# Attention, gated layers and a SiLU layer on one core: sums, low halves and normalising of the opening moved to GpSimd, with a new opening order

## The chip, the cores and the metric

One core of a Trainium2 chip. The metric is the device time in microseconds (us) of one execution, from its first to its last instruction with what lies around it. The engines are TensorE (PE, with its weight loads PEld), VectorE (DVE), ScalarE (ACT), GpSimd (POOL) and SyncE (SP), which issues the loads and stores.

## The reference

Three stages in a row, all in 32-bit floats. B = 4, H = 8 heads, S = 576 positions, head size 64.

```python
# 1. attention
q_d, k_d, v_d = means over 4 neighbouring positions of q, k, v     # 144 positions
out_d     = softmax(q_d @ k_d.T / 8) @ v_d                          # coarse
scores    = where(|i - j| < 4, q @ k.T / 8, -1e9)
out_local = softmax(scores) @ v                                     # local
x = (repeat(out_d, 4) + out_local)        # reshaped to 2304 tokens x 512
# 2. gated layer: w1, w2 512 x 1024, w3 1024 x 1024, w_out 1024 x 512
x = ((x @ w1) * (x @ w2)) @ w3 @ w_out
# 3. SiLU layer: w_in 512 x 2048, w_out 2048 x 512
h = x @ w_in;  y = (h * sigmoid(h)) @ w_out
```

Softmax subtracts the row's maximum and divides by the sum plus 1e-9.

## The kernel before

**Units.** The attention is done in 16 units u, each one batch entry and a pair of heads. A unit loads its q and k (`qk`, 579 KB, L289), a version of v cut into windows (`vw`, two loads, 200 and 160 KB, L296) and v for the coarse part (`vr`, 320 KB, L302). Its steps have names in the order list, the unit's number last:
- coarse part: `pq` sums q and k over four positions (DVE, L309); `sd` scores (PE, L351); `md` negated maximum (DVE, L359, L361); `xd` three exponentials (ACT, L323) into tile Ed; `rd` the inverse of the sums (DVE, two small steps, L330 and L333); `nd` normalising of Ed (L338 on ACT or L340 on GpSimd); `td0`, `td1` transposes (PE, L401); `cd` copies of them (ACT); `pv0`, `pv1` v's pooled sums (L437, L444); `od` the product with v (PE, L453); `os` its copy out of PSUM (DVE, L461).
- local part: `s` scores of 64 queries by 38 keys, 72 small products in the records (PE, L376); `mk` adds the mask (DVE, L386) into the one tile `band`; `ml` the maximum (DVE, L390) and its scaled negative (L392); `x0` to `x2` nine exponentials (ACT, L323); `rl` inverse (DVE); `n0` to `n2` normalising of band; `tl0` to `tl2` transposes (PE, L423) and `cl` copies; `ol` the product with the windows of v (PE, L475).
- `xf` adds the two (DVE, L488), `xh` takes the high half of the sum as FP32R (ACT, L501) and `xo` subtracts it to get the low half (L505): products of the later stages are made of passes over high and low halves.

**Weights.** w3 and w_out are not applied one after the other: their product is made first, in 64 products `pGHT` of 128x128 by 128x512 (PE, L592, tiles `wp`; two records each in the trace), and cast into w_wC (L601, L606). Weights lie in memory as 64-bit floats. Each piece (`o0` to `o3` of w_out, `t00` to `t13` of w3, `w12_0` to `w12_7` of w1 and w2 side by side) is loaded in two halves of 512 KB (`Lw...`, L221) and decoded in four steps: `a` on ACT (L174, 0.67 us for half a piece), `d1` clamp (DVE, L179), `d2` shift (DVE, L185), `d3` join (DVE, L191). A w12 piece then gets a high half (`h`, ACT, L265) and a low half (`l`, DVE, L268), tiles w_wA and w_wB.

**Opening.** Units 0 to 4 and most of unit 5, the 64 products, the decoding and the first products of the gated layer (`ab`, L640) stand in one list, `OPENING`, written out by hand (L38 to L71): each engine, and SP with its loads, works off its own instructions in this order, one after the other. At most eight loads are on their way at once. While the list runs, `side()` is DVE and `norm` works slice by slice on ACT; behind it `side()` is GpSimd, and `norm` is one GpSimd instruction. So in the opening GpSimd has nothing to do after making the mask. `KEYS` is the order in which the weight pieces claim buffers, `CUTS` the pieces whose first parts are cut smaller. Idle products (L126) on a zeroed tile stand ahead of everything on PE (NWARM of them) and, as `z0` and `z1`, in the list.

**After the opening** the units 6 to 15 are interleaved with the gated layer, and then the SiLU layer runs over all tokens. The change touches there only `mk`, `ml` and the scale of `x0` to `x2`.

Of the kernel before, what the change touches and what calls it, by code (L numbers as in the profile page):

```python
# [35 lines left out]


OPENING = """  # L38
Lwt000 Lwt001 Lwt002 Lq0 Lwo00 Lwo01 Lwt010 Lwt011 at00a d2t00a Lwo10 d1t00a Lwo11 at00b d3t00a
d2t00b d1t00b d3t00b Lva0 at00c d2t00c d1t00c d3t00c Lvb0 s0 pq0 Lr0 ao0a d2o0a sd0 z0 z1 mk0  # L40
ml0 Lq1 ao0b d1o0a d3o0a x00 md0 p000 Lwo20 x10 d1o0b p001 d2o0b xd0 d3o0b Lq2 p002 d2t01 x20
p003 rd0 Lwo21 at01 rl0 p004 p005 nd0 d1t01 Lwt020 p006 d3t01 Lwt021 n00 Lwo30 td00 n10 d2o1
td10 Lwo31 p007 n20 pv00 ao1 pv10 Lwt030 pq1 s1 cd00 cd10 tl00 tl10 d1o1 Lr1 cl00 sd1 cl10 d3o1
tl20 od0 Lwt031 cl20 md1 p010 os0 xd1 pq2 p011 Lq3 ao2 p012 d2o2 Lwt100 p013 rd1 mk1 nd1 p014
d1o2 Lwt101 d3o2 sd2 at02 d2t02 s2 Lww12_00 md2 p015 d1t02 p016 Lww12_01 d3t02 ao3 p017 ml1 ol0
Lq4 d1o3 x01 Lwt110 p020 pv01 x11 pv11 p021 d2o3 Lva1 x21 d3o3 p022 at03 p023 rl1 Lr2 d2t03 p024
n01 d1t03 n11 p025 d3t03 Lvb1 n21 p026 pq3 p027 Lwt111 p030 d2t10 at10 xf00 p031 Lww12_20 xf10
xh00 td01 d1t10 xh10 td11 cd01 d3t10 Lww12_21 p032 cd11 xd2 tl01 d2w12_0 tl11 p033 xo00 cl01 rd2
cl11 tl21 xo10 aw12_0 p034 mk2 ml2 od1 cl21 wh00 d1w12_0 p035 nd2 wl00 p036 os1 wh01 d3w12_0
p037 x02 ol1 wl01 wh02 wh03 pv02 p100 x12 wl02 Lva2 Lvb2 wl03 p101 x22 xf01 p102 xf11 hw12_0 rl2  # L50
td02 pv12 td12 n02 d2t11 Lr3 p103 n12 lw12_0 p104 n22 d2w12_2 sd3 xh01 xh11 xo01 cd02 s3 xo11
cd12 md3 tl02 at11 Lq5 tl12 pq4 p105 cl02 p106 cl12 aw12_2 d1t11 tl22 d3t11 od2 cl22 xd3 p107
os2 Lwt120 d1w12_2 p110 Lwt121 d3w12_2 sd4 rd3 ol2 Lww12_30 hw12_2 mk3 Lww12_31 ml3 nd3 p111
lw12_2 Lva3 Lvb3 x03 p112 xf02 p113 x13 xf12 pv03 td03 x23 d2t12 td13 p114 pv13 at12 md4 Lr4
p115 rl3 xh02 d1t12 s4 xh12 n03 d3t12 p116 Lq6 n13 p117 xo02 Lwt130 n23 xo12 Lwt131 p120 d2w12_3
cd03 cd13 pq5 p121 xd4 tl03 tl13 pv04 aw12_3 p122 rd4 p123 cl03 d1w12_3 cl13 nd4 tl23 d3w12_3
od3 p124 cl23 os3 Lww12_10 hw12_3 mk4 p125 Lww12_11 ml4 at13 p126 lw12_3 p127 x04 d1t13 ol3 x14
d2t13 d3t13 x24 sd5 Lva4 Lvb4 pv14 s5 Lww12_50 rl4 Lr5 xf03 aw12_1 p130 Lq7 d2w12_1 Lww12_51
td04 xf13 n04 p131 d1w12_1 n14 d3w12_1 td14 n24 p132 md5 cd04 p133 Lww12_40 cd14 Lww12_41 hw12_1
tl04 tl14 p134 cl04 lw12_1 cl14 tl24 xh03 p135 wh10 xo03 cl24 od4 mk5 wh11 wl10 p136 xh13 aw12_5  # L60
wl11 p137 os4 xo13 wh12 ab000a d1w12_5 wh13 ab000b wl12 xd5 ab000c wl13 ab001a af00 d2w12_5
ab001b aw12_4 ab001c d3w12_5 ab010a ab010b cf00 Lww12_60 hw12_5 ab010c cc00 Lww12_61 d1w12_4
ab011a co00 af01 ab011b lw12_5 ab011c ab020a d2w12_4 ab020b cf01 ab020c cc01 ab021a d3w12_4 af02
co01 ab021b ab021c rd5 Lww12_70 hw12_4 d2w12_6 ab030a Lww12_71 cf02 ab030b aw12_6 cc02 ab030c
lw12_4 co02 ab031a nd5 ab031b d1w12_6 af03 ab031c d3w12_6 ab040a ab040b cf03 ab040c hw12_6 cc03
ab041a ml5 co03 ab041b af04 lw12_6 aw12_7 ab041c ab050a x05 cf04 ab050b cc04 ab050c x15 d1w12_7
co04 ab051a d2w12_7 af05 ab051b x25 d3w12_7 ab051c ab060a cf05 ab060b hw12_7 cc05 ab060c rl5
ab061a co05 af06 lw12_7 ab061b n05 ab061c n15 ol4 cf06 n25 cc06 ab070a co06 Lva5 xf04 ab070b
Lvb5 xf14 xh04 ab070c xh14 xo04 ab071a af07 xo14 ab071b ab071c ab100a cf07 ab100b cc07 ab100c
ab101a co07 af10 ab101b ab101c cf10 cc10 co10  # L70
""".split()  # L71


# [1107 lines left out]
```

## Time and profile before

| | |
|---|---|
| median of 3 runs | 843.88 us (843.46 to 847.28) |
| profiled execution, its own time | 843.95 us |
| its span in the trace | 842.1 us |
| granted TensorE clock, mean | 1.00 (2.4 GHz) |
| PE busy | 831.4 us, 99% of the span |
| DVE, ACT, GpSimd busy | 494.7, 304.0, 270.7 us |

The trace is of one execution. "Busy" counts the time in which an engine works on an instruction, waiting left out; what an engine waits for is in the views of waits, and in square brackets behind a row of the timeline. Times on the axis count from the span's start.

### The profile page before, as it was taken

The page shows a single profiled execution, that of the slowest core. Times are in us where ns is not written, and L with a number is a line of the kernel's source. Part 1 is how long each engine was busy: PE and PEld are TensorE (multiplying, and loading weights), DVE is VectorE, ACT ScalarE, POOL GpSimd, SP SyncE. Part 2 cuts the span into 40 slices and gives each one's busy share as a digit, 9 for nine tenths or more (in the row PEclk, how much of TensorE's full clock was granted, in tenths as well). Part 3 has the DMA queues.
Part 4 walks back from the last instruction along what each step waited for, and adds up shares of the span by engine and source line. Part 5 has one row for each costly group of instructions (what it writes and reads, how often), then busy time and mean ns, then how long its engine had stood idle before and what let it go on. Part 6 is the DMA issues. An engine that isn't in the chain of part 4 may idle for free.

```text
span 842.1 us, 17446 instructions
## 1 busy us (share of the span) xinstructions
PE 831.4 (99%) x7126; PEld 737.6 (88%) x7126; DVE 494.7 (59%) x833; ACT 304.0 (36%) x881; POOL 270.7 (32%) x216
## 2 busy tenths in 40 slices
PE   8999999999999999999999999999999999999997
PEld 4555798999999999999999998999999998988986
DVE  7999896666455737356952543447544537534434
ACT  6598665544444435433432111123111123211111
POOL 3000233453434534231451432435232435221220
PEclk9999999999999999999999999999999999999999
DMA  9978755446455543518951783542762432832502
GB/s 312 378 196 262 228 169 166 143 154 225 159 206 170 192 168 106 200 59 288 369 197 35 282 302 140 182 181 87 214 199 88 148 115 87 236 102 89 168 6 76
DMA packets 44032, 149.16 MB, mean 177 GB/s; under 512 B 9136, under 2 KB 15792, under 8 KB 37808
## 3 DMA queue, kind: packets, MB, share of 16 engines
q1 hardware_dynamic: 43952, 148.05, 52.0%
q8 instruction: 56, 0.92, 0.5%
q14 instruction: 24, 0.20, 0.1%
HBM read 115.52 MB, written 32.51 MB: 176 GB/s over the span
## 4 chain that ended last, share of the span: by engine, by line
PE 94%; DMA 3%; DVE 2%; issue 0%; SPq 0%; ACT 0%
PE o L986 24%; PE ab L640 23%; PE h L1075 21%; PE y L705 12%; PE wp L592 5%; PE ol L475 2%; PE sd L351 1%; PE tl L423 1%; PE s L376 1%; DMA qk<-qk 1%; PE td L401 1%; PE od L453 1%; DMA st<-w 1%; DMA lent<-wo 1%; DVE w_wA L268 0%
## 5 line engine op out<-in xcount | busy, mean ns | idle before, releaser
L986 PE MATMUL o<-wo,g 128*128 128x512 f32 x864 | 221.1, 393 | 0.0
L986 PEld LDWEIGHTS o<-wo,g 128*128 128x128 f32 x864 | 160.7, 188 | 25.4
L1039 POOL TENSOR_TENSOR g<-sg,g 128x768 fp32r<-128x768 f32 x46 | 84.9, 1846 | 228.4 <-DVE g L1037 217.3
L1075 PE MATMUL h<-yc,wcb 128*128 128x384 f32 x576 | 116.1, 337 | 0.0
L1075 PEld LDWEIGHTS h<-yc,wcb 128*128 128x128 f32 x576 | 103.2, 188 | 7.7
L705 PE MATMUL y<-c,w_wC 128*128 128x320 f32 (+1 forms) x768 | 109.2, 297 | 0.0
L640 PE MATMUL ab<-x,w_wB 128*128 128x320 f32 (+1 forms) x768 | 109.1, 297 | 0.0
L680 POOL TENSOR_TENSOR c<-cf,c 128x320 fp32r<-128x320 f32 (+1 forms) x64 | 74.1, 1158 | 106.7 <-DVE c L675 100.5
L640 PE MATMUL ab<-x,w_wA 128*128 128x320 f32 (+1 forms) x768 | 105.8, 295 | 1.2 <-DVE w_wA L268 1.2
L640 PEld LDWEIGHTS ab<-x,w_wB 128*128 128x128 f32 x768 | 102.4, 188 | 1.7 <-issue 1.0
L640 PEld LDWEIGHTS ab<-x,w_wA 128*128 128x128 f32 x768 | 101.6, 188 | 2.1 <-DVE w_wA L268 1.5
L705 PEld LDWEIGHTS y<-c,w_wC 128*128 128x128 f32 x768 | 102.3, 188 | 1.3 <-issue 1.0
L1028 ACT ACTIVATE sg<-cf 128x768 f32<-128x768 f32 x24 | 20.3, 847 | 182.8 <-DVE cf L1063 182.8
L1075 PE MATMUL h<-yc,wca 128*128 128x384 f32 x432 | 83.1, 336 | 0.0
L1075 PEld LDWEIGHTS h<-yc,wca 128*128 128x128 f32 x432 | 76.6, 188 | 3.8
L656 DVE TENSOR_TENSOR cf<-ab,af 128x320 f32<-128x320 f32 (+1 forms) x64 | 29.0, 454 | 56.3 <-PE ab L640 43.9
L592 PE MATMUL wp<-w_wo,w_w 128*128 128x512 f32 x128 | 60.1, 602 | 0.5 <-DVE w_wo L191 0.4
L437 POOL TENSOR_TENSOR vr<-vr 72x512 f32<-72x512 f32 x11 | 16.8, 1525 | 116.0 <-DMA vr<-vr 116.0
L1028 ACT ACTIVATE sg<-cg 128x768 f32<-128x768 f32 x24 | 20.3, 847 | 88.2 <-DVE cg L1063 88.2
L1063 DVE TENSOR_TENSOR u<-h,u 128x384 f32<-128x384 f32 x48 | 26.6, 554 | 39.2 <-PE h L1075 39.0
L323 ACT ACTIVATE band<-band,sml 128x38 f32<-128x38 f32 x144 | 45.0, 319 | 3.9 <-DVE sml L392 3.9
L650 ACT COPY af<-ab 128x320 f32<-128x320 f32 (+1 forms) x64 | 25.4, 397 | 54.3 <-PE ab L640 54.3
(118 smaller groups left out, 1006.2 us busy)
## 6 DMA issues: line engine op xcount, KB each, us to landing
wcb<-wsd SPq DMA_DIRECT2D x24, 1024.0 KB
wca<-wsd SPq DMA_DIRECT2D x24, 768.0 KB
sw<-wb SPq DMA_DIRECT2D x32, 512.0 KB
qk<-qk SPq DMA_DIRECT2D x16, 579.0 KB
wsd<-res SPq DMA_DIRECT2D x8, 1024.0 KB
wod<-res SPq DMA_DIRECT2D x8, 1024.0 KB
wo<-wod SPq DMA_DIRECT2D x8, 1024.0 KB
st<-w SPq DMA_DIRECT2D x14, 512.0 KB
```

The source lines that it names most:

```text
L323: nc.scalar.activation(E[:, j, :], src[:, j, :], AF.Exp, bias=z[:, j:j + 1], scale=scale, accum_out=z[:, NQB + j:NQB + j + 1],)
L592: nc.tensor.matmul(wp_ps[half, j], lhsT=w3v[:, k, j * P:(j + 1) * P], rhs=wov[:, k, :], start=(gp == 0 and k == 0), stop=(gp == 3 and k == 1),
L640: nc.tensor.matmul(acc[:, :N], lhsT=wv[:, i, w, kk, :], rhs=X[b, h, kk][:, j, :], start=(n == 0), stop=(n == 11),)
L650: mark(nc.scalar.copy(af, C.pop(("ab", b, h, m, 0))[:, :N]))
L656: nc.vector.tensor_tensor(out=cf, in0=C.pop(("ab", b, h, m, 1))[:, :N], in1=C.pop(("af", b, h, m)), op=ALU.mult)
L680: mark(nc.gpsimd.tensor_tensor(out=c[:, 1], in0=C.pop(("cf", b, h, m)), in1=c[:, 0].bitcast(F32), op=ALU.subtract))
L705: nc.tensor.matmul(acc[:, :N], lhsT=WP[kf // 2][:, i, kf % 2, ec * P:(ec + 1) * P], rhs=c[:, j, :], start=(kf == 0 and n == 0), stop=(kf = ...
L986: nc.tensor.matmul(acc, lhsT=g[:, a, j * P:(j + 1) * P], rhs=w[:, b, half, :], start=(p == 0 and half == 0 and n == 0), stop=(p == 7 and h ...
L1028: nc.scalar.activation(sg, c, AF.Sigmoid)
L1039: e.tensor_tensor(out=g[:, 1], in0=sg, in1=g[:, 0].bitcast(F32), op=ALU.subtract)
L1063: nc.vector.tensor_tensor(out=out_, in0=in0, in1=in1, op=op)
L1075: nc.tensor.matmul(acc, lhsT=wc[w][:, a, c, kt * P:(kt + 1) * P], rhs=y[:, b, kt, :], start=(n == 0), stop=(n == 5),)
```

## The change

- `mk` scales the scores by 0.125 and adds the mask in one instruction, the mask's low value is -1e9 in place of -8e9, and the exponentials take the scale 1.0.
- `ml` writes the negated maximum straight away, so that its second instruction is gone, in all 16 units.
- In the opening GpSimd does `pv0`, `pv1`, `xo` (before: DVE) and both normalisings, one instruction each (before: three and nine slices on ACT; `n1` and `n2` are gone). The copy `os` goes from DVE to ACT there.
- NWARM goes from 9 to 4; the list has four idle products instead of two.
- `OPENING`, `KEYS` and `CUTS` are laid out anew.

```diff
-NEG = -8.0e9
-NWARM = 9
+NEG = -1.0e9
+NWARM = 4
...
-KEYS = [('w3', (0, 0)), ('wo', 0), ('w3', (1, 0)), ('wo', 1), ('wo', 2), ...
+KEYS = [('w3', (0, 0)), ('wo', 0), ('w3', (1, 0)), ('wo', 1), ('w3', (2, 0)), ...
-CUTS = {('wo', 0): [(0, 0, 512), (1, 0, 512)], ('w3', (0, 0)): [(0, 0, 256), (0, 256, 512), (1, 0, 512)]}
+CUTS = {('wo', 0): [(0, 0, 512), (1, 0, 512)], ('w3', (0, 0)): [(0, 0, 128), (0, 128, 512), (1, 0, 512)]}
...
-    def side():
-        return nc.vector if opening[0] else nc.gpsimd
...
-        def norm(z, E, n, width, lo, hi):
-            if opening[0]:
-                for j in range(lo, hi):
-                    nc.scalar.mul(E[:, j, :], E[:, j, :], z[:, NQB + j:NQB + j + 1])
-            elif lo == 0:
-                nc.gpsimd.tensor_tensor(
-                    out=E, in0=E, op=ALU.mult,
-                    in1=z[:, NQB:NQB + n].unsqueeze(2).to_broadcast([P, n, width]),
-                )
+        def norm(z, E, n, width):
+            nc.gpsimd.tensor_tensor(
+                out=E, in0=E, op=ALU.mult,
+                in1=z[:, NQB:NQB + n].unsqueeze(2).to_broadcast([P, n, width]),
+            )
...
         def local_mask():
-            nc.vector.tensor_tensor(out=EL, in0=hold["s"], in1=mask, op=ALU.add)
+            nc.vector.scalar_tensor_tensor(
+                out=EL, in0=hold["s"], scalar=0.125, in1=mask, op0=ALU.mult, op1=ALU.add
+            )

         def local_max():
-            m = att.tile([P, NQB], F32, tag="ml", name=f"ml{u}")
-            nc.vector.tensor_reduce(out=m, in_=EL, axis=AX.X, op=ALU.max)
             hold["zl"] = small("sml")
-            nc.vector.tensor_scalar(
-                out=hold["zl"][:, 0:NQB], in0=m, scalar1=-0.125, scalar2=None, op0=ALU.mult
+            nc.vector.tensor_reduce(
+                out=hold["zl"][:, 0:NQB], in_=EL, axis=AX.X, op=ALU.max, negate=True
             )
...
-            side().tensor_tensor(
+            nc.gpsimd.tensor_tensor(
                 out=r[:, :, 0:2, :], in0=r[:, :, 0:2, :], in1=r[:, :, 2:4, :], op=ALU.add
             )
...
-            nc.vector.tensor_copy(hold["od"], hold["acc"][:, :SD])
+            if opening[0]:
+                nc.scalar.copy(hold["od"], hold["acc"][:, :SD])
+            else:
+                nc.vector.tensor_copy(hold["od"], hold["acc"][:, :SD])
```

`pool_v1` and `x_rest` change as `pool_v0` does. The lines of the changed kernel stand 1 to 8 above those of the kernel before (L437 is L429, L505 is L500, L340 is L332, L423 is L415).

**The first loads on SP's queue.** lent and st are raw weights, with the source behind the arrow.

Before:

```order
L221 DMA lent_135<-w3t 128x512 x2
L221 DMA lent_135<-w3t 128x1024
L289 DMA qk0_139<-qk 128x1158
L221 DMA lent_141<-wo 128x1024 x2
L221 DMA lent_144<-w3t 128x1024 x2
L221 DMA lent_150<-wo 128x1024 x2
L296 DMA vw0_159<-vw 40x1280
L296 DMA vw0_159<-vw 40x2x512
L302 DMA vr0_205<-vr 80x1024
L289 DMA qk1_224<-qk 128x1158
```

After:

```order
L285 DMA qk0_130<-qk 128x1158
L220 DMA lent_132<-w3t 128x256
L220 DMA lent_134<-wo 128x1024
L220 DMA lent_132<-w3t 128x768
L292 DMA vw0_137<-vw 40x1280
L292 DMA vw0_137<-vw 40x2x512
L220 DMA lent_132<-w3t 128x1024
L220 DMA lent_134<-wo 128x1024
L220 DMA lent_142<-w3t 128x1024 x2
L220 DMA lent_187<-wo 128x1024 x2
L285 DMA qk2_209<-qk 128x1158
L285 DMA qk1_212<-qk 128x1158
```

qk0 went from the fourth place to the first, the two window loads of v from behind the second wo piece to ahead of the second half of the first; qk2 came in ahead of qk1, and vr0 left for a later place.

**GpSimd's queue.** Before, the first instructions behind the making of the mask belong to unit 5:

```order
L145 MEMSET mask_89 32x3
L437 TENSOR_TENSOR vr5_1177<-vr5_1177 72x2x256
L444 TENSOR_TENSOR vd5_1736<-vr5_1177 72x256
L437 TENSOR_TENSOR vr6_1738<-vr6_1738 72x2x256
L680 TENSOR_TENSOR c0_0_0_1332<-cf0_0_0_1322,c0_0_0_1332 128x320
```

After, the piece of it around unit 2 (band is the local part, sml its sums; the third band row below is unit 2's):

```order
L332 TENSOR_TENSOR band_90<-band_90,sml_428 128x9x38
L500 TENSOR_TENSOR x0_0_521<-xf0_0_481,x0_0_521 128x320
L500 TENSOR_TENSOR x0_1_528<-xf0_1_513,x0_1_528 128x256
L429 TENSOR_TENSOR vr2_515<-vr2_515 72x2x256
L436 TENSOR_TENSOR vd2_610<-vr2_515 72x256
L332 TENSOR_TENSOR Ed2_616<-Ed2_616,smd_595 128x432
L429 TENSOR_TENSOR vr3_620<-vr3_620 72x2x256
L500 TENSOR_TENSOR x1_0_690<-xf1_0_678,x1_0_690 128x320
L500 TENSOR_TENSOR x1_1_702<-xf1_1_686,x1_1_702 128x256
L332 TENSOR_TENSOR band_90<-band_90,sml_608 128x9x38
```

Ahead of the normalising of unit 2's band now stand unit 3's first sum of v and unit 1's two low halves.

**PE's queue around the transposes of unit 2.** Before:

```order
L401 MATMUL td2_0_720<-ident_84,Ed2_599 72x128 x3
L401 MATMUL td2_1_726<-ident_84,Ed2_599 72x128 x3
L592 MATMUL wp1_3_736<-w_wo_207,w_w3_569 128x512
L592 MATMUL wp1_0_694<-w_wo_207,w_w3_569 128x512
L351 MATMUL sd3_747<-qkd3_563 64x144 x6
L376 MATMUL s3_761<-qk3_395 32x38 x36
L423 MATMUL tl2_0_806<-ident_84,band_90 102x128 x2
```

After:

```order
L393 MATMUL td2_0_693<-ident_84,Ed2_616 72x128 x3
L393 MATMUL td2_1_698<-ident_84,Ed2_616 72x128 x3
L587 MATMUL wp1_2_704<-w_wo_202,w_w3_476 128x512
L587 MATMUL wp1_3_713<-w_wo_202,w_w3_476 128x512
L587 MATMUL wp1_0_674<-w_wo_202,w_w3_476 128x512
L587 MATMUL wp1_1_684<-w_wo_202,w_w3_476 128x512
L587 MATMUL wp1_2_704<-w_wo_202,w_w3_476 128x512
L415 MATMUL tl2_0_735<-ident_84,band_90 102x128 x2
```

Between td2 and tl2 there are five products of the weights now, in the place of two products and the scores of unit 3.

## Rows read from the trace of the kernel before

**Rows 1.** The page's first part: busy us (share of the span) xinstructions.

```profile
PE 831.4 (99%) x7126; PEld 737.6 (88%) x7126; DVE 494.7 (59%) x833; ACT 304.0 (36%) x881; POOL 270.7 (32%) x216
```

**Rows 2.** PE's waits, whole span: us in total, times, longest us.

```profile
PE s L376 <- DMA qk<-qk: 1.4, 2, 1.2
PE spare L126 <- DVE zero L122: 1.3, 1, 1.3
PE ab L640 <- DVE w_wA L268: 1.2, 1, 1.2
...
PE tl L423 <- ACT ET L430: 0.2, 1, 0.2
```

**Rows 3.** Windows: us, busy of PE, PEld, DVE, ACT, POOL, clock, DMA share, GB/s.

```profile
40.00:60.00 20.00, 20.00 (x218) 10.75 (x217) 18.56 (x36) 17.01 (x62) 0.00 (x0) 1.00 0.76 221
...
10.00:15.00 5.00, 4.56 (x22) 2.56 (x23) 4.83 (x12) 4.21 (x24) 0.00 (x0) 1.00 1.02 404
15.00:20.00 5.00, 5.00 (x17) 2.29 (x15) 3.44 (x8) 5.00 (x18) 0.00 (x0) 1.00 1.04 257
```

**Rows 4.** Timeline of PE, start: start us, us, what [idle before <-releaser]; second row from 5.62.

```profile
1.29 6.67 PE L126 MATMUL spare<-zero 128*128 128x288 f32 x18 [1.29 <-DVE zero L122]
...
5.62 2.35 PE L126 MATMUL spare<-zero 128*128 128x288 f32 x9
8.15 0.85 PE L376 MATMUL s<-qk 64*32 64x38 f32 x72 [0.19 <-DMA qk<-qk]
...
12.51 6.28 PE L592 MATMUL wp<-w_wo,w_w 128*128 128x512 f32 x14 [0.44 <-DVE w_wo L191]
18.63 0.82 PE L401 MATMUL td<-ident,Ed 128*72 128x128 f32 x6
...
21.48 0.85 PE L376 MATMUL s<-qk 64*32 64x38 f32 x72 [1.17 <-DMA qk<-qk]
```

**Rows 5.** Timelines of ACT and DVE: second half of wo o0, and an inverse.

```profile
10.67 0.67 ACT L174 ACTIVATE w_wo<-lent 128x512 f32<-128x512 f32 x1 [0.62 <-DMA lent<-wo]
...
11.31 0.42 DVE L179 TENSOR_SCALAR w_wo<-w_wo 128x512 f32<-128x512 f32 x1
...
13.88 0.70 DVE L191 SCALAR_TENSOR_TENSOR w_wo<-w_wo,lent 128x512 int32<-128x512 int32 x1
...
15.72 0.21 DVE L333 RECIPROCAL sml<-sml 128x9 f32<-128x9 f32 x1
```

**Rows 6.** GpSimd's lines by form, whole span: xcount | busy us, mean ns | idle before.

```profile
L505 POOL TENSOR_TENSOR x<-xf,x 128x320 fp32r<-128x320 f32 x11 | 9.7, 886 | 18.3 <-ACT x L501 18.3
...
L340 POOL TENSOR_TENSOR Ed<-Ed,smd 128x432 f32<-128x432 f32 x10 | 9.1, 908 | 30.1 <-DVE smd L333 17.7 <-DVE sml L392 12.4
...
L505 POOL TENSOR_TENSOR x<-xf,x 128x256 fp32r<-128x256 f32 x11 | 8.3, 759 | 2.6 <-ACT x L501 2.6
L340 POOL TENSOR_TENSOR band<-band,sml 128x342 f32<-128x342 f32 x10 | 7.6, 765 | 14.7 <-DVE sml L333 14.7
```

**Rows 7.** DVE's lines by form, 0 to 100 us.

```profile
L437 DVE TENSOR_TENSOR vr<-vr 72x512 f32<-72x512 f32 x5 | 3.4, 684 | 2.0 <-DMA vr<-vr 1.9
...
L505 DVE TENSOR_TENSOR x<-xf,x 128x256 fp32r<-128x256 f32 x4 | 2.4, 605 | 0.0
...
L505 DVE TENSOR_TENSOR x<-xf,x 128x320 fp32r<-128x320 f32 x4 | 1.9, 486 | 0.2 <-ACT x L501 0.2
...
L392 DVE TENSOR_SCALAR sml<-ml 128x9 f32<-128x9 f32 x5 | 0.9, 173 | 0.2
```

**Rows 8.** Timeline of DVE and GpSimd around 99.5 us.

```profile
99.45 1.23 DVE L191 SCALAR_TENSOR_TENSOR dec<-dec,st 128x1024 int32<-128x1024 int32 x1
99.48 2.35 POOL L437 TENSOR_TENSOR vr<-vr 72x512 f32<-72x512 f32 x1 [3.84 <-DMA vr<-vr]
```

**Rows 9.** Lines L437 and L330: ns min/median/max, first and last start, form.

```profile
L437 POOL TENSOR_TENSOR vr<-vr x11: 1270/1290/2354, 93.5 to 312.6; 72x512 f32<-72x512 f32 x11
...
L330 DVE TENSOR_SCALAR smd<-smd x16: 157/168/850, 15.1 to 344.1; 128x3 f32<-128x3 f32 x16
```

More of the change, by code (lines that the diff above doesn't have):

```diff
@@ L38 @@
 OPENING = """
[L39 to L68, printed above, removed]
@@ L69 @@
-Lvb5 xf14 xh04 ab070c xh14 xo04 ab071a af07 xo14 ab071b ab071c ab100a cf07 ab100b cc07 ab100c
-ab101a co07 af10 ab101b ab101c cf10 cc10 co10
+Lq0 Lwt000 Lwo00 Lwt001 Lva0 Lvb0 Lwt002 Lwo01 Lwt010 pq0 s0 Lwt011 at00a d1t00a Lwo10 d2t00a
+sd0 z0 z1 z2 z3 d3t00a ao0a d2o0a mk0 Lwo11 at00b d2t00b Lq2 d1o0a Lq1 d1t00b d3t00b d3o0a
+Lwt020 at00c d2t00c p000 md0 Lwt021 d1t00c ao0b d3t00c xd0 p001 d1o0b Lr0 d2o0b d3o0b Lwo20 p002
+rd0 at01 d2t01 nd0 ml0 p003 Lwo21 d1t01 x00 td00 d3t01 td10 Lwo30 cd00 p004 ao1 d2o1 p005 Lwo31
@@ new lines @@
+cd10 p006 d1o1 x10 d3o1 p007 Lwt030 x20 s1 pq1 Lwt031 p010 rl0 p011 Lwt100 at02 d2t02 n00 sd1
+Lwt101 pv00 d1t02 tl00 tl10 Lww12_60 pq2 cl00 p012 cl10 pv10 tl20 Lq3 d3t02 p013 ao2 od0
+Lww12_61 d2o2 cl20 p014 os0 d1o2 p015 Lr1 d3o2 ao3 p016 d2o3 Lwt110 p017 d1o3 p020 Lwt111 d3o3
+at03 p021 d2t03 Lww12_10 p022 d1t03 p023 d3t03 Lww12_11 p024 d2t10 p025 md1 p026 mk1 xd1 ml1
+p027 x01 rd1 ol0 d2w12_6 nd1 at10 p030 Lva1 xf00 pv01 x11 Lvb1 d1t10 p031 d3t10 x21 td01 pv11
+p032 aw12_6 rl1 sd2 xf10 Lr2 n01 cd01 d2t11 xh00 td11 d1w12_6 xh10 tl01 xo00 cd11 s2 pq3 cl01
@@ new lines @@
+tl11 aw12_1 xo10 Lq4 tl21 d3w12_6 p033 pv02 cl11 p034 cl21 md2 hw12_6 od1 mk2 p035 wh00 ml2 pv12
+lw12_6 os1 p036 xd2 Lr3 p037 wl00 wh01 ol1 wh02 rd2 wl01 wh03 nd2 wl02 x02 p100 Lva2 xf01 Lvb2
+x12 p101 xf11 pv03 wl03 xh01 td02 d1w12_1 td12 xh11 p102 cd02 xo01 d2w12_1 cd12 d3w12_1 p103 x22
+xo11 p104 at11 rl2 Lwt120 p105 Lwt121 n02 hw12_1 d1t11 p106 d3t11 tl02 tl12 cl02 sd3 lw12_1 cl12
+Lww12_20 Lww12_21 tl22 pq4 od2 cl22 s3 os2 pv13 md3 p107 Lq5 mk3 Lr4 xd3 p110 ml3 d2t12 p111 x03
+rd3 sd4 d2w12_2 x13 nd3 p112 x23 md4 p113 pq5 aw12_2 pv04 s4 at12 rl3 p114 Lq6 d1w12_2 n03 p115
@@ new lines @@
+d3w12_2 p116 d1t12 Lwt130 hw12_2 p117 Lwt131 d3t12 ol2 lw12_2 Lww12_30 p120 Lww12_31 Lva3 xf02
+p121 Lvb3 xf12 xh02 xh12 td03 xo02 td13 cd03 p122 xd4 xo12 d2t13 tl03 p123 cd13 rd4 cl03 tl13
+at13 nd4 tl23 p124 mk4 cl13 ml4 p125 cl23 aw12_3 d1t13 od3 d3t13 x04 p126 pv14 d1w12_3 p127 x14
+Lww12_00 Lww12_01 d2w12_3 p130 Lr5 x24 d3w12_3 p131 os3 rl4 Lww12_40 hw12_3 ol3 n04 Lww12_41
+lw12_3 p132 Lva4 Lvb4 p133 xf03 aw12_0 xf13 p134 d2w12_0 xh03 p135 d1w12_0 wh10 xo03 p136
+d3w12_0 xh13 wh11 xo13 p137 wh12 wl10 Lww12_70 hw12_0 td04 Lww12_71 wl11 td14 sd5 wl12 wh13 cd04
@@ new lines @@
+lw12_0 s5 cd14 aw12_4 tl04 Lq7 wl13 tl14 ab000a d2w12_4 cl04 ab000b cl14 d1w12_4 ab000c d3w12_4
+ab001a aw12_7 ab001b md5 ab001c af00 Lww12_50 hw12_4 Lww12_51 ab010a d1w12_7 ab010b cf00 xd5
+ab010c cc00 lw12_4 ab011a co00 af01 ab011b ab011c rd5 d2w12_7 ab020a nd5 cf01 ab020b cc01 ab020c
+aw12_5 d3w12_7 co01 ab021a ab021b af02 d2w12_5 ab021c hw12_7 d1w12_5 ab030a cf02 ab030b cc02
+ab030c lw12_7 ab031a co02 af03 ab031b d3w12_5 ab031c ab040a cf03 ab040b hw12_5 cc03 ab040c co03
+ab041a af04 lw12_5 ab041b ab041c tl24 cf04 od4 cl24 cc04 ab050a os4 mk5 co04 ab050b ml5 ab050c
@@ L71 @@
+x05 ab051a ab051b af05 x15 ab051c ab060a cf05 x25 ab060b cc05 ab060c co05 rl5 ab061a af06 ab061b
+n05 ab061c ab070a cf06 ab070b cc06 ab070c co06 ab071a af07 ab071b ab071c ab100a cf07 ab100b cc07
+ab100c ab101a co07 af10 ab101b ab101c ol4 cf10 cc10 co10 Lva5 xf04 Lvb5 xf14 xh04 xh14 xo04 xo14
 """.split()
@@ L274, in weight_ops @@
         op("l" + name, rest)
-    KEYS = [('w3', (0, 0)), ('wo', 0), ('w3', (1, 0)), ('wo', 1), ('wo', 2), ('w3', (2, 0)), ('wo', 3), ('w3', (3, 0)), ('w3', (0, 1)), ('w12', 0), ('w3', (1, 1)), ('w12', 2), ('w3', (2, 1)), ('w12', 3), ('w3', (3, 1)), ('w12', 1), ('w12', 5), ('w12', 4), ('w12', 6), ('w12', 7)]
-    CUTS = {('wo', 0): [(0, 0, 512), (1, 0, 512)], ('w3', (0, 0)): [(0, 0, 256), (0, 256, 512), (1, 0, 512)]}
+    KEYS = [('w3', (0, 0)), ('wo', 0), ('w3', (1, 0)), ('wo', 1), ('w3', (2, 0)), ('wo', 2), ('wo', 3), ('w3', (3, 0)), ('w3', (0, 1)), ('w12', 6), ('w3', (1, 1)), ('w12', 1), ('w12', 2), ('w3', (2, 1)), ('w3', (3, 1)), ('w12', 3), ('w12', 0), ('w12', 4), ('w12', 7), ('w12', 5)]
+    CUTS = {('wo', 0): [(0, 0, 512), (1, 0, 512)], ('w3', (0, 0)): [(0, 0, 128), (0, 128, 512), (1, 0, 512)]}
     for n, key in enumerate(KEYS):
@@ L443, in pool_v1 @@
             t = att.tile([HD, 2, P], F32, tag="vd", name=f"vd{u}", bufs=1)
-            side().tensor_tensor(out=t, in0=r[:, :, 0, :], in1=r[:, :, 1, :], op=ALU.add)
+            nc.gpsimd.tensor_tensor(out=t, in0=r[:, :, 0, :], in1=r[:, :, 1, :], op=ALU.add)
             hold["vd"] = t
@@ L504, in x_rest @@
             x = X[u // 4, h, u % 4]
-            side().tensor_tensor(
+            nc.gpsimd.tensor_tensor(
                 out=x[:, 1], in0=hold["xf", h], in1=x[:, 0].bitcast(F32), op=ALU.subtract
@@ L512, in unit_ops @@
         op("rd" + U, lambda: inverse(hold["zd"], 3, 0.25))
-        op("nd" + U, lambda: norm(hold["zd"], hold["Ed"], 3, SD, 0, 3))
+        op("nd" + U, lambda: norm(hold["zd"], hold["Ed"], 3, SD))
         op("s" + U, local_scores)
@@ L517, in unit_ops @@
         for k in range(3):
-            op(f"x{k}" + U, lambda k=k: exps(hold["zl"], EL, EL, 3 * k, 3 * k + 3, NQB, 0.125))
-            op(f"n{k}" + U, lambda k=k: norm(hold["zl"], EL, NQB, KW, 3 * k, 3 * k + 3))
+            op(f"x{k}" + U, lambda k=k: exps(hold["zl"], EL, EL, 3 * k, 3 * k + 3, NQB, 1.0))
             op(f"tl{k}" + U, lambda k=k: local_turn(k))
@@ L522, in unit_ops @@
         op("rl" + U, lambda: inverse(hold["zl"], NQB, 1.0))
+        op("n0" + U, lambda: norm(hold["zl"], EL, NQB, KW))
         for h in range(2):
@@ L541, in tile_model @@
         unit_ops(u)
-    for k in range(2):
+    for k in range(4):
         op(f"z{k}", idle_product)
@@ L553, in scores @@
             f"sd{u} md{u} xd{u} rd{u} nd{u} s{u} mk{u} ml{u} x0{u} x1{u} x2{u} rl{u} "
-            f"n0{u} n1{u} n2{u} Lq{u + 2}"
+            f"n0{u} Lq{u + 2}"
         )
```

## Prediction

> **What bounds the kernel now.** I read the engines' totals first, then PE's waits, then the opening in time. PE is busy for 831.4 of 842.1 us [rows 1]. What it waited for from outside is a short list [rows 2]: 1.4 us for loads of q and k, 1.3 for the zeroed tile at the very start, 1.2 for w_wA, 0.2 for a copy on ACT, and little else. From 40 to 60 us DVE is 93% busy and ACT 85%, GpSimd does nothing, and yet PE has no gap [rows 3]. So what DVE and ACT are spared there is worth nothing by itself, while anything newly late on GpSimd is paid in full. Only the start holds something to win [rows 4]: PE spends 1.29 to 8.0 us on idle products, starts the first local scores at 8.15, the first wp product at 12.51, and the second unit's scores at 21.48, after 1.17 us of waiting for qk1. Behind that only the waits for w_wA and for the copy are left.
>
> All sums are made against the profiled execution, 843.95 us (span 842.1, 1.9 around it); the median of the three runs is 843.88, so the same to 0.1. A measurement of this kernel can tell about 0.5%, 4.2 us: faster means under 839.7, slower over 848.1.
>
> **The start, step by step.** qk0 is now the first load, and four idle products instead of nine stand ahead of it: their eight records, at the 0.48 us of the first ones [rows 4], end at 5.1. So s0 starts near 5.1 instead of 8.15, and p000 near 10.4 instead of 12.51 (wo's first half is the third load instead of the fifth, 2.1 us at 1.28 a load and with qk0 ahead). A gain of 3 us would last only if the next links came earlier too. They don't:
> - The second half of wo o0 has the same 2,627 KB of loads ahead of it as before, when it landed at 10.67 [rows 5], but v's two window loads have been put ahead of it. In the 5 us in which these moved before, the rate was 257 GB/s against 404 in the 5 us ahead [rows 3]: 0.735 MB less, 1.8 us, and their own 360 KB take 0.9. So it lands near 10.67 + 2.7 = 13.3.
> - On DVE, rd0 stands behind that half's decoding: 13.3 + 0.67 (ACT) + 0.42 + 0.42 + 0.70 [rows 5] + 0.35 for rd0's two steps = 15.9. Then nd0, now one GpSimd instruction of 0.91 [rows 6], which I let meet DVE for 0.5 (below): td0 at 17.3. It was 18.63.
> - PE has only p000 to p003 for this time, 4 x 0.87 from 10.4 (0.87 is the 14 records, 7 products, from 12.51 to 18.63), and is through at 13.9. It waits some 3.4 us.
> - Then td0 (0.82) and p004 to p007 (3.5) stand ahead of s1: 21.6. Before, three of these four ran ahead of td0, in its shadow, and s1 waited for qk1 anyway. qk1 is the 14th load in both orders; qk2 (579 KB) is now ahead of it in the place of vr0 (320 KB): 259 KB at 404 GB/s is up to 0.6 us later.
>
> So s1 starts 0.1 to 0.6 us later than before, and the whole head start is gone. I take **+0.2**.
>
> **GpSimd's new work.** The built program gives GpSimd 32 more TENSOR_TENSORs (10 of v's pooled sums, 10 low halves, 6 + 6 normalisings); DVE loses 41 instructions, ACT 72. What they cost on either engine is in the trace, since the later units do the same on GpSimd: the sum of vr takes 1.29 [rows 9] against 0.68 on DVE, the two low halves 0.89 and 0.76 against 0.49 and 0.6, the normalisings 0.91 and 0.77 [rows 6, 7]. If all that is longer lay on PE's path, it would be (0.61 + 0.4 + 0.15) x 5 units = 5.8 us for these three. The Trainium skill, GPSIMD Engine Reference, section 4.1 "Engine selection", gives elementwise work on two inputs to VectorE, GpSimd being about twice as slow; the rule speaks against this change, and the vr sum (1.9 times) bears it out. How much does lie on the path is read from the order.
>
> The queue in front of tl2, shown above, is the dearest place. Let DVE's join (L190) begin at 0. PE has td2 behind it and five products, and stands ready at 2.77. GpSimd's queue holds the sum of vr3 (whose load lands at 0.58), two low halves of x, and only then the normalising that tl2 needs: from 0.58, 1.29 + 0.89 + 0.76 + 0.77 = 3.7, so 4.3. PE waits 1.5. Before, the normalising was on ACT and none of this stood in the queue.
>
> **Do the two engines slow each other?** The trace shows one clear pair: a DVE join began at 99.45 and took 1.23; GpSimd's sum is shown from 99.48 and took 2.35 instead of its usual 1.29 [rows 8, 9]. It ended at 101.83; started at the join's end, 100.68, it would have ended at 101.97. In the other direction L330, 0.157 at best, once took 0.85 [rows 9]. I therefore let a GpSimd TENSOR_TENSOR and a DVE instruction with two SBUF inputs, or a DVE pass from SBUF to SBUF, go one after the other. The Trainium skill, SBUF — State Buffer, "SBUF: two separate sides", states this as an exclusive lock on a port pair that the two share; by that rule tl2 waits the longer time below, without it the shorter one above, and this pair of rows agrees with it. With the blocking, at tl2: the join ends at 1.23, the sum at 2.4; the inverse's first step, behind the sum, at 2.4, its reciprocal (0.21 [rows 5]) at 2.6; the first low half at 3.2; the second beside a clamp at 4.4; the next join has the normalising wait, which ends at 6.1. PE waits 3.4 instead of 1.5.
>
> I laid the whole new order out in time in this way with the rows' durations. Behind s1 PE waits: 0.7 for od0 (vr0 is now the 17th load instead of the 13th), 1.3 before the two halves of td1, 1.3 for tl1 (the same queue as tl2's, shorter), 3.4 for tl2, 1.1 for a product near 80 us whose weights wait behind a blocked join, 0.8 for a window of v, 1.5 for w_wA, and 1.6 in eight or more short ones: 11.7. The same walk through the old order gives 4.9, where the trace has 1.4 from s1 on (1.2 for w_wA, 0.2 for the copy [rows 2]). So the walk is too dark by 3.5. If it errs equally in both, the change costs 11.7 - 4.9 = **+6.8**, which I take; if its error is proportional, 11.7 x 1.4/4.9 - 1.4 = +1.9; if it errs in the old order alone, 11.7 - 1.4 = +10.3. Without the mutual blocking the walk gives +2.7.
>
> **Costed at nothing**: the 16 instructions of 0.17 saved at the negated maximum [rows 7], the 9 us of sums and low halves that DVE is spared (5 x 1.77) and ACT's normalisings, because PE hardly waits for either in the old order [rows 2]; the scaled mask step, the same pass in another form; the copy of the coarse result on ACT, which is less full now. If this cover failed, the worst would be one such step a unit in PE's way, 5 x 0.5 us. The idle products stand in PE's waiting time at the start.
>
> Sum: 843.95 + 0.2 + 6.8 = **851.0 us**.
>
> **Rivals.**
> 1. *The start is kept* (faster). If s1 can start 3.15 us earlier, at 18.3, and PE then never waits for GpSimd, the gain of s0 goes through and the 1.2 us for w_wA, whose decoding has a freer DVE, goes too: 843.95 - 3.15 - 1.2 = 839.6. It decides at td0: it would have to start by 14.0, before nd0's inverse has even come up behind the decoding at 15.5. Against it: qk1's place in the loads [rows 4] and rd0's place in DVE's queue. For it: my walk is too dark in the old order, and GpSimd has whole free stretches [rows 3]. Chance 0.13.
> 2. *GpSimd's steps hide* (same). If the two engines rarely meet, the +2.7 holds: 846.8; if the error of the walk is proportional, 846.1. For it: later units' normalisings keep to 0.91 and 0.77 on average [rows 6]. Against it: DVE is over 90% busy here, so they will meet. Chance 0.22.
> 3. *PE's clock falls in the new wait* (slower still). At the start of the program nine records of idle products took 4.33 us where the next nine took 2.35 [rows 4], so products after a standstill went at about half the pace, 2.0 us lost, although the granted clock of the profile read 1.00. If the 3.4 us ahead of td0 bring this back, 851.0 + 2.0 = 853.0. The Trainium skill, TensorE: Matmul & The Clock Gate, Part 1, calls the lower level the state without activity. Against it: no row of the old start shows that pace again behind a pause, though those pauses, 0.19 to 0.44 us [rows 4], were far shorter. Chance 0.08.
>
> That the change does not do what it says is excluded by the built program's counts.
>
> **How the numbers follow.** Forecast 0.57 at 851.0, with its own range from 848.2 to 854.5 (the walk's ends, less likely outwards). Slower by over 0.5% is the forecast and rival 3: 0.65; the same is rival 2: 0.22; faster is rival 1: 0.13. The range leaves out rival 1 and a little at the top, some 2 in 10: 844.0 to 855.5.
>
> **What would show it.** Right: s0 near 5.1 and s1 near 21.5; PE waiting about 3 us ahead of td0 for Ed and several us for GpSimd's band and Ed between 40 and 70 us; L429 and L500 on GpSimd at 1.5 us and more where DVE joins run. Wrong: s1 well before 20, tl's and td's waits for GpSimd under 1 us in all, or PE as unbroken from 25 to 110 us as before.

## The result and the profile after

The changed kernel takes 857.86 us (median of 4 runs, 856.63 to 859.49); the kernel before, in the same comparison, 845.58 (843.46 to 850.23). The ratio is 1.0139, with a 95% interval of 1.0089 to 1.0188. The forecast was slower, 851.0, with a range from 844.0 to 855.5: the direction came, the size did not; the median lies 2.4 us above the range.

The profiled execution of the changed kernel took 859.49 us, 15.5 more than that of before. Its first part of the page, to be held against [rows 1]:

```profile
PE 838.2 (98%) x7120; PEld 740.1 (86%) x7120; DVE 486.2 (57%) x792; ACT 288.0 (34%) x814; POOL 304.9 (36%) x248
```

DVE and ACT have 41 and 67 instructions less in the page (ACT 72 slices of normalising less, five copies more), GpSimd 32 more. But PE, which does the same products (less six records of idle ones), is busy for 6.8 us longer. The waits of PE, against [rows 2]:

```profile
PE wp L587 <- DVE w_w L190: 3.3, 1, 3.3
PE od L445 <- POOL vd L436: 2.3, 1, 2.3
PE td L393 <- POOL Ed L332: 2.3, 1, 2.3
PE wp L587 <- DVE w_wo L190: 1.8, 1, 1.8
PE tl L415 <- POOL x L500: 1.7, 1, 1.7
PE spare L125 <- DVE zero L121: 1.3, 1, 1.3
PE tl L415 <- POOL band L332: 0.8, 1, 0.8
PE ab L635 <- DVE w_wA L267: 0.6, 1, 0.6
```

They sum to 14.1 us, the old list to 5.4 (the four of [rows 2], and two more, given here): 8.7 more.

```profile
PE sd L351 <- DVE qkd L309: 0.9, 1, 0.9
PE wp L592 <- DVE w_wo L191: 0.4, 1, 0.4
```

8.7 and 6.8 make up the whole 15.5. The windows, with the columns of [rows 3], show where PE is busy for longer:

```profile
20.00:40.00 20.00, 17.67 (x123) 8.08 (x122) 13.94 (x18) 7.27 (x20) 4.19 (x3) 0.83 1.03 362
80.00:100.00 20.00, 16.71 (x145) 8.69 (x138) 14.93 (x22) 10.71 (x38) 5.09 (x6) 0.91 0.64 208
100.00:120.00 20.00, 18.23 (x173) 15.61 (x173) 16.67 (x24) 12.42 (x27) 7.53 (x6) 0.91 0.58 193
```

The granted clock is under 1.00 in just these three; the rest up to 850 us has 1.00, as the profiled execution of the old kernel has up to 830 (behind that PE runs out of work, with the clock at 0.89 and 0.98). (0.17 + 0.09 + 0.09) x 20 = 7.0 us of full pace are missing; inside them the clock stands at its lower level, 0.50 (1.2 GHz), as from 32 to 36 us. The 6.8 us are a net figure: up to the second unit's scores PE is busy for 1.2 us less (fewer idle products), behind them for 8.1 more. So some 1 us of that is not the clock's; where it comes from stays open. The timeline of PE shows each fall close behind a standstill:

```profile
5.43 1.15 PE L368 MATMUL s<-qk 64*32 64x38 f32 x72
...
11.40 3.70 PE L587 MATMUL wp<-w_wo,w_w 128*128 128x512 f32 x8 [1.80 <-DVE w_wo L190]
17.38 0.85 PE L393 MATMUL td<-ident,Ed 128*72 128x128 f32 x6 [2.28 <-POOL Ed L332]
18.07 3.60 PE L587 MATMUL wp<-w_wo,w_w 128*128 128x512 f32 x8
21.59 0.85 PE L368 MATMUL s<-qk 64*32 64x38 f32 x72
...
30.16 1.23 PE L445 MATMUL od<-EdT,vd 72*64 72x144 f32 x8 [2.31 <-POOL vd L436]
31.32 13.29 PE L587 MATMUL wp<-w_wo,w_w 128*128 128x512 f32 x24
...
66.06 0.65 PE L415 MATMUL tl<-ident,band 128*102 128x128 f32 x4 [0.78 <-POOL band L332]
...
83.79 2.98 PE L587 MATMUL wp<-w_wo,w_w 128*128 128x512 f32 x4 [3.29 <-DVE w_w L190]
86.56 1.48 PE L393 MATMUL td<-ident,Ed 128*72 128x128 f32 x6
...
107.00 0.74 PE L415 MATMUL tl<-ident,band 128*102 128x128 f32 x4 [1.68 <-POOL x L500]
107.49 16.20 PE L635 MATMUL ab<-x,w_wB 128*128 128x320 f32 x96
```

Behind the stop of 2.31 us ahead of od0, twelve products take 13.29 us in place of 12 x 0.87 = 10.5, and od0 itself 1.23 in place of 0.71. Behind 3.29 us near 80 us, two products take 2.98 in place of 1.9 and the transposes 1.48 in place of 0.82. Behind 1.68 us ahead of unit 4's tl the low clock falls on the products of the gated layer (`ab`). Behind the stop of 2.28 us ahead of td0 nothing of the kind happens: the four products there keep their 3.6 us.

### The profile page after: what moved, and what is told of

It is laid out like the page before. It is cut to its first block, busy times and chain, and to the rows that moved or that the text cites. A ratio compares the mean times of both kernels' runs of the same rounds, so it can differ in the third digit from the quotient of the medians.

```text
span 857.7 us, 17381 instructions
## 1 busy us (share of the span) xinstructions
PE 838.2 (98%) x7120; PEld 740.1 (86%) x7120; DVE 486.2 (57%) x792; ACT 288.0 (34%) x814; POOL 304.9 (36%) x248
## 4 chain that ended last, share of the span: by engine, by line
PE 85%; DMA 6%; DVE 5%; ACT 1%; POOL 1%; issue 1%; SPq 1%; ACTq 0%; POOLq 0%
PE o L981 23%; PE ab L635 21%; PE h L1070 21%; PE y L700 12%; DMA st<-w 3%; PE ol L470 2%; PE wp L587 2%; DMA vr<-vr 1%; PE tl L415 1%; PE sd L343 1%; DVE dec L190 1%; DMA lent<-w3t 1%; PE od L445 1%; PE s L368 1%; DMA qk<-qk 1%; PE td L393 1%
## 5 line engine op out<-in xcount | busy, mean ns | idle before, releaser
L587 PE MATMUL wp<-w_wo,w_w 128*128 128x512 f32 x128 | 63.5, 635 | 5.1 <-DVE w_w L190 3.3
L587 PEld LDWEIGHTS wp<-w_wo,w_w 128*128 128x128 f32 x128 | 24.0, 201 | 29.4 <-issue 22.4
```

Source lines behind the costliest of these rows:

```text
L587: nc.tensor.matmul(wp_ps[half, j], lhsT=w3v[:, k, j * P:(j + 1) * P], rhs=wov[:, k, :], start=(gp == 0 and k == 0), stop=(gp == 3 and k == 1),
```

## The experiments

The profile names GpSimd (Ed, vd, x, band) as often as DVE. My first theory (B) was that of the prediction, GpSimd's slower steps; its rival (A) was the new order, whoever does the steps. A third question was the clock: C, it falls because PE stands idle, and the time is lost; D, it falls for another reason, or later waits hide the loss. The kernel before took 845.58 us in the comparison above and 843.93, 843.61 or 845.43 in those below, so versions from different comparisons are held against each other by their ratio to it.

**The mask step alone.**

```diff
 kernel before
-NEG = -8.0e9
+NEG = -1.0e9
-            nc.vector.tensor_tensor(out=EL, in0=hold["s"], in1=mask, op=ALU.add)
+            nc.vector.scalar_tensor_tensor(
+                out=EL, in0=hold["s"], scalar=0.125, in1=mask, op0=ALU.mult, op1=ALU.add)
...
+                out=hold["zl"][:, 0:NQB], in_=EL, axis=AX.X, op=ALU.max, negate=True
```

> The kernel before with the scaled mask step and the negated maximum alone. Both theories (A, the new order makes the loss; B, GpSimd's slower steps make it) expect no change against before, within 2 us of it: 16 instructions of 0.17 us go from DVE, for which PE hardly waits. If the new form of the mask step were dear, PE would wait for it and the time would rise by some us.

844.94 us against 843.93, ratio 1.0011 (0.9985 to 1.0037): no change, as both expected. The step of the prediction that costed it at nothing holds.

**All the moves between engines, in the old order.**

```diff
 kernel before with the mask step
     def side():
-        return nc.vector if opening[0] else nc.gpsimd
+        return nc.gpsimd
...
+        def norm(z, E, n, width):     # one instruction on GpSimd, as in the changed kernel
...
+            if opening[0]:
+                nc.scalar.copy(hold["od"], hold["acc"][:, :SD])
```

> The order, loads and cuts of before, with all that the change gives to other engines: v's pooled sums, low halves and both normalisings on GpSimd, the copy of the coarse result on ACT, the new mask step. A (the order): 1 to 3 us over before, since the old order has room for the slower steps and no wait long enough to bring the clock down. B (GpSimd): most of the loss of the changed kernel, 9 us or more over before, with the waits of PE for tiles of GpSimd.

846.82 us against 843.93, ratio 1.0026 (1.0006 to 1.0046): 2 to 3 us. A's number came, B's did not. GpSimd's sums and DVE's passes do hold each other up here, as the lines by form from 0 to 110 us show (1.29 and 0.89 are the free durations of the first two, 0.68 that of the third):

```profile
L432 POOL TENSOR_TENSOR vr<-vr 72x512 f32<-72x512 f32 x7 | 11.4, 1631 | 16.0 <-DMA vr<-vr 14.6 <-PE wp L590 1.4
L503 POOL TENSOR_TENSOR x<-xf,x 128x320 fp32r<-128x320 f32 x4 | 5.8, 1453 | 11.2 <-ACT x L499 11.2
```

```profile
L184 DVE TENSOR_SCALAR lent<-lent 128x1024 int32<-128x1024 int32 x6 | 6.2, 1041 | 0.7 <-DMA lent<-w3t 0.4 <-issue 0.3
```

But no wait of PE names a tile of GpSimd; the longest are 1.4 us for qk and 1.2 for w_wA, both there before, and one of 0.7 for w_wC is new.

**The new order alone.**

```diff
 changed kernel
+    def side():
+        return nc.vector if opening[0] else nc.gpsimd
...
+            if opening[0]:
+                for j in range(lo, hi):
+                    nc.scalar.mul(E[:, j, :], E[:, j, :], z[:, NQB + j:NQB + j + 1])
```

> The changed kernel's order, loads and cuts, with v's pooled sums, low halves and the copy of the coarse result back on DVE and the normalisings slice by slice on ACT. A (the order): stays 8 us or more over before, with PE waiting 2 us or more for the first Ed and again for a product near 80 us. B (GpSimd): back to before, within 3 us.

855.64 us against 843.93, ratio 1.0124 (1.0085 to 1.0162). Nearly the whole loss is there with the old engines. PE waits nearly as long (12.1 us in all against 14.1), only for others, and the clock falls here too, to 0.83 from 30 to 40 us behind the stop of 3.0:

```profile
PE tl L422 <- ACT band L337: 3.0, 1, 3.0
PE td L400 <- ACT Ed L337: 1.8, 1, 1.8
PE tl L422 <- ACT EdT L411: 1.7, 1, 1.7
PE wp L591 <- DVE w_wo L190: 1.7, 1, 1.7
```

So A holds in this sense: the order loses with either set of engines, and the moves between engines cost little in the old one. It is not the same stops that come back. The first Ed is waited for 1.8 us, just under the 2 expected; the product near 80 us only 0.5; and the 3.0 us for band belong to this mixture, since the new list has one place for normalising it, where ACT now does nine slices in a row. In the changed kernel's own stops GpSimd does have a part: ahead of the product near 80 us two of DVE's passes take 1.54 and 1.67 us, where their kind takes 0.68 and 1.22 alone, and ahead of od0 GpSimd's two sums take 1.64 and 1.79, against 1.29 and 0.84 in the old kernel (median and mean). Giving the steps back removes these stops and puts ACT's in their place.

**The clock: idle products in the stops.**

```diff
 changed kernel; idle products write columns of the tile that the kernel does not use
+            if u == 0:                       # ahead of od0: 4
+                for _ in range(4):
+                    nc.tensor.matmul(acc[:, 144:432], lhsT=ident, rhs=mflat[:, 0:288],
+                                     start=True, stop=True)
...
+        if u == 4: op("fi4", lambda: fill(10))    # ahead of p120
+        if u == 5: op("fi5", lambda: fill(5))     # behind s5
```

> The changed kernel with 4, 10 and 5 idle products put into three of PE's waits (ahead of the first od, of product p120, and behind the scores of unit 5); nothing else moves. Theory C, that the clock falls because PE stands idle there and costs 6.8 us of the loss: the granted clock stays at 1.00 behind these places and the time falls by 4 to 7 us against the changed kernel. Rival D, that the clock falls for another reason or that what it costs is hidden behind waits that follow anyway: the clock or the time stays as in the changed kernel, within 2 us.

856.24 us, ratio 1.0140 (1.0101 to 1.0180): no gain over the changed kernel's 1.0139, a miss for C as it was put. The trace shows why. At all three filled places the clock read 1.00. But in this execution the unfilled stop ahead of td0 was 3.8 us long, and the clock fell there:

```profile
18.58 1.50 PE L407 MATMUL td<-ident,Ed 128*72 128x128 f32 x6 [3.80 <-POOL Ed L332]
19.86 5.79 PE L606 MATMUL wp<-w_wo,w_w 128*128 128x512 f32 x8
```

The four products there took 5.79 us; in the changed kernel's own profile, behind 2.28 us of waiting, 3.60. So that stop was filled as well:

```diff
+            if u == 0 and kh == 0:
+                for _ in range(9):
+                    nc.tensor.matmul(tp[:, 384:512], lhsT=ident, rhs=mflat[:, 0:128], ...)
```

> The changed kernel with idle products in four of PE's waits: the three of the run before and nine ahead of the first unit's coarse transposes, where the clock fell in that run. Theory C (the clock follows PE's standstills and what it takes is lost): the granted clock stays at 1.00 from 10 to 120 us, and the time is 852 to 854 us, since the waits themselves remain. Rival D (the clock's loss is hidden by later waits): 856 us or more at a clock of 1.00.

The clock of all windows is 1.00 in the profiled execution, which took 853.26 us, as C said; the median of four is 855.5 (853.26 to 857.37, mean clocks of 0.997 to 0.999), between what C and D expected. The nearest reading of the stops without the clock is this one execution: 9.3 us over the profiled one of before. Against its own comparison the ratio is 1.0139 (1.0110 to 1.0168), the same as the changed kernel's, though the plain medians are 2.4 us apart. So the clock follows the stops, as C says; that filling them makes the changed kernel faster in the median is not shown.

**A stop by itself.** To see the price of one standstill in a kernel that has none of this length, GpSimd was given memsets to do behind v's first sum, and PE a small product of their result ahead of od0:

```diff
 kernel before with the mask step
+                nc.gpsimd.tensor_copy(late[:HD, 0:1], r[:, 0, 0, 0:1])
+                for _ in range(11):
+                    nc.gpsimd.memset(late, 0.0)
...
+                for _ in range(FILL):       # 0, or 5 idle products
+                    nc.tensor.matmul(acc[:, 144:432], lhsT=ident, rhs=flat[:, 0:288], ...)
+                nc.tensor.matmul(acc[:, 144:272], lhsT=ident, rhs=late[:, 0:128], ...)
```

> The kernel before with the new mask step, plus one made-up stop: ahead of the first od PE gets a product that needs a tile which GpSimd finishes near 26.4 us, so that PE stands still for some 2.4 us near 24 us; no other work moves. Theory C: the stop costs its 2.4 us, less up to 1 us of a wait for w_wA near 110 us that it covers, and in most executions the granted clock falls behind it for 6 us or so, another 3 us: 846 to 850 us with a clock under 1.00 in most. Rival D (a single stop of this length leaves the clock alone, or the loss is made good later): 844 to 847 us at a clock of 1.00.

> The same stop with five idle products (2.6 us) in it, so that PE works until the tile is there. Theory C: the clock stays at 1.00 from 20 to 40 us, and the time is 2 to 3 us under that of the unfilled stop, 844 to 847 us. Rival D: the same time as the unfilled stop, within 1 us.

The memsets took longer than I had worked out, and the stop ended at 27.81 in both. Unfilled:

```profile
27.81 0.49 PE L461 MATMUL od<-late,ident 128*128 128x128 f32 x2 [3.75 <-POOL late L445]
28.23 1.14 PE L467 MATMUL od<-EdT,vd 72*64 72x144 f32 x8
29.30 5.78 PE L606 MATMUL wp<-w_wo,w_w 128*128 128x512 f32 x10
35.01 0.95 PE L352 MATMUL sd<-qkd 64*64 64x144 f32 x12
```

Filled with 2.6 us of idle products:

```profile
27.81 0.49 PE L461 MATMUL od<-late,ident 128*128 128x128 f32 x2 [1.21 <-POOL late L445]
28.23 0.71 PE L467 MATMUL od<-EdT,vd 72*64 72x144 f32 x8
28.87 4.56 PE L606 MATMUL wp<-w_wo,w_w 128*128 128x512 f32 x10
33.36 0.95 PE L352 MATMUL sd<-qkd 64*64 64x144 f32 x12
```

The same stop, and 1.65 us later at the next scores; the granted clock was 0.92 from 20 to 30 us and 0.91 from 30 to 40 in the one, 1.00 in the other. The medians are 850.80 (9 runs) and 849.28 (12 runs) against 845.43: 1.5 us apart, where C expected 2 to 3 and D at most 1. The means are 2.1 apart, with a standard error of 0.7, so the difference is clear of the noise. Here two versions of the same comparison differ by the idle products, and so by the clock, alone. A stop costs about its length (849.28 - 845.43 = 3.85 us, the stop was 3.8), and the low clock behind it comes on top. Of the 1.65 us, 1.5 are left at the end of the two profiled executions (850.01 and 848.53); nothing later made it good.

**Can the stops be taken out?** Three edits of the order:

```diff
 loads: first loads as before      Lwo11 Lva0 Lvb0 Lr0 ... Lq1 Lq2
 t12:   decoding of t12 first      d1t12 d3t12 d1w12_2 ... d3w12_2
 all:   both, and                  td04 cd04 ... td14 cd14
```

> The changed kernel with its first fifteen loads in the order of before: v's windows behind the second wo piece, vr0 next, qk1 ahead of qk2. If the order of the loads made the stops at the start: the first coarse transposes start near 16 us instead of 17.4, the wait of 2.3 us for vd0 goes and with it the low clock behind it, and a wait of about 1.5 us for qk1 comes up; 4 to 6 us less than the changed kernel. If GpSimd's own queue made them, od still waits for vd and the time stays within 2 us.

857.49 us, ratio 1.0148 (1.0119 to 1.0177), no gain. The expected steps did come: td0 at 16.62, a wait of 0.9 us for qk1, od0 at 28.43 without a wait. The first ol started 4.8 us earlier than in the changed kernel (39.75 against 44.54). But the product near 80 us waited 3.1 us again and started at 82.00 against 83.79: it hangs on the decoding of its weights, not on PE.

> The changed kernel with DVE decoding the w3 piece t12 ahead of the w12_2 piece, and nothing else. If its place behind w12_2 made the stop of 3.3 us near 80 us: that wait and the low clock behind it go (5 us), a wait of up to 2 us for Ed comes up a little later, 2 to 5 us less than the changed kernel. If late loads or blocking by GpSimd made it, the product waits on and the time stays.

857.09 us, ratio 1.0156 (1.0126 to 1.0187), no gain. The product waits 0.6 us now, but the transposes behind it took over, and here the stop ahead of td0 was of the long kind (rows from the waits):

```profile
PE td L393 <- POOL Ed L332: 4.1, 1, 4.1
PE td L393 <- DVE xf L483: 2.7, 1, 2.7
```

> Both moves together, and the copies of unit 4's coarse transposes on ACT right behind them, ahead of the casts of wp. If the order is the whole cause, the three great stops and their low clock go: 846 to 850 us. If something else holds PE up, 853 or more.

855.22 us, ratio 1.0132 (1.0104 to 1.0161), against 1.0139 no clear gain, and far from the 846 to 850 expected. Its profiled execution had a clock of 1.00 in every window to 140 us, and still took 854.40: its waits sum to 14.0 us, as in the changed kernel, in fourteen entries instead of eight. So none of these edits took the stops out: what was taken away at one place stood up at the next. That PE is ahead of what DVE, GpSimd and the loads can deliver in this order is my reading of it; no run takes it apart.

**The head start by itself.**

```diff
 kernel before with the mask step
-NWARM = 9
+NWARM = 4
+Lq0 moved ahead of Lwt000
```

> The kernel before with the new mask step, four idle products instead of nine and qk0 as the first load, as the changed kernel starts: is the head start of the first scores worth anything by itself? If qk1's place as the 14th load sets the second unit's scores, s0 starts near 5 us, s1 near 21.4 us as before, and the time is that of before within 2 us. If a head start carries through (the rival by which the change would have been faster), 841 us or less.

847.78 us, ratio 1.0016 (0.9999 to 1.0034). No gain, though 2.4 us over before where within 2 was said, and not in the way that I said: PE then waits 6.3 us for the pooled qk0, which stands behind the decoding on DVE, the clock is 0.59 from 10 to 20 us, and s1 starts at 24.63 instead of 21.4. Of these 3.2 us only some 2 reach the end; the waits for qk1 and for w_wA are gone from its list. Whether qk1 alone would have held s1 back stays open.

No version ran faster than the kernel before.

## Why the prediction was partly right

- **The start** holds closely: td0 at 17.38 (forecast 17.3), s1 at 21.59 (21.6), with the wait for wo's second half that the moved window loads cause. p000 started at 11.40, 1 us later than said, and the wait ahead of td0 was 2.3 instead of 3.4. The term of +0.2 measured +0.1.
- **The sum of the stops behind s1** was well sized: 3.3 + 2.3 + 1.7 + 0.8 + 0.6 = 8.7 us, less 1.4 before, is +7.3, where +6.8 stood. It was badly placed. tl2, the dearest place of the forecast, cost 0.8 instead of 3.4; od0 2.3 instead of 0.7, the product near 80 us 3.3 instead of 1.1, and 1.7 at unit 4's tl came from nowhere on the list. GpSimd's queue ahead of tl2 was as slow as worked out (its sum began at 59.45, the normalising ended at 66.00), but PE came there later: its five products ended 5.8 us behind that sum's start, where the walk had 2.2. Nor was blocking what made the queue slow: the sum took 1.27 us, and 2.1 of the 6.5 were spent waiting for ACT's high half and DVE's inverse.

```profile
59.45 1.27 POOL L429 TENSOR_TENSOR vr<-vr 72x512 f32<-72x512 f32 x1
61.30 2.13 POOL L500 TENSOR_TENSOR x<-xf,x 128x320 fp32r<-128x320 f32 x2 [0.57 <-ACT x L496]
64.98 1.02 POOL L332 TENSOR_TENSOR band<-band,sml 128x342 f32<-128x342 f32 x1 [1.55 <-DVE sml L329]
```

- Of the other places on the forecast's list, the 1.3 us each for tl1 and for td1's halves didn't come, and of the sign "several us between 40 and 70 us" only 0.8 did. That the sum is right with its places wrong is luck.
- **The cause was named wrongly in the main.** "GpSimd's new work" and "do the two engines slow each other" were argued as the reason, and the rules cited there were read as speaking for it. The moves between engines alone cost 0.06 to 0.46%, the order alone 0.85 to 1.62%. The blocking is there (GpSimd's first sum takes 1631 ns on average in the old order with GpSimd at work), but the old order has room for it. What the prediction read from GpSimd's queue, it should also have asked of the old engines in the same order.
- **The step that failed** is the one that let products behind a stop run at full pace. The clock stood in the text only as rival 3, with a chance of 0.08, at one place (td0) and with 2.0 us; the sum has no term for it. In the profiled execution it fell at three other places and took some 7 of the 15.5 us, so that PE was busy behind s1 for 8.1 us more, where the sum has 0. How much of the median's 857.86 it makes is open. The mean granted clock of the four runs is 0.991, 0.994, 0.997 and 0.994; but the kernel before pays for it too in some executions: in the 51 of the comparisons above its mean clock goes from 0.993 to 1.000 (median 0.999), and the five at 0.993 and 0.994 took 849.1 to 851.1 us, the twelve at 1.000 a median of 843.9. So, by these means, the new order adds to such falls and does not begin them; why they come in the old one, no trace here shows. The Trainium skill, TensorE: Matmul & The Clock Gate, Part 1, which the rival cited, calls the lower level the state without activity; the three falls behind stops, to 0.50, agree with it, though not every stop brought one (last section).
- Rival 1 (the start is kept) is refuted by s1, rival 2 (the steps hide) by the stops.

## What to carry to other kernels

Where one engine runs back to back and the others are nearly full too, a new order should be judged by the stops it gives that engine, with the engines as they were and as they will be; which engine does a small step may matter less than where the step stands in the queue. Count each stop of TensorE twice: its length, and a chance (here behind stops of 1.25 to 6.3 us, not behind all) that products close behind it run at half pace for some us. Taking away one stop was worth nothing clear in the three edits here: the next one grew.

## What the runs showed that I had not expected

- Whether the clock falls does not follow from the length of the one stop. It fell behind 1.25 us (ahead of tl1 with the old loads: two products then took 3.11 us instead of 1.88), and stayed at 1.00 behind 2.28 (td0 in the changed kernel) and behind 2.71 (unit 3's transposes with all three edits). Behind the same stop of 2.71 with t12's decoding alone it fell: the transposes took 1.21 us instead of 0.82. Behind 3.75, 3.80 and 4.1 it fell each time.
- In the changed kernel a fall cost 1.8 to 3.4 us of full pace (the windows above), so it lasted some 3.5 to 7 us. At the start of the program nine records of idle products ran at half pace while the granted clock read 1.00 [rows 4]; behind the stops the clock showed it.
- The same stop differs between executions of kernels with the same start: td0 waited 2.3, 3.8 and 4.1 us, as the second half of wo came at 13.2 us in the changed kernel, at 14.4 in the one with three fills and at 14.1 in the one with t12 first.
